# GpSimd's order around the first norm: the second value-weight load ahead of the power, two casts behind the next pair's x

## The chip, the cores and the metric

The kernel runs on one core of a Trainium2 chip. The metric is the device time of one execution in microseconds. A core has five engines with a queue of instructions each, worked off in order: TensorE (PE, with its weight loads as PEld), VectorE (DVE), ScalarE (ACT), GpSimd (POOL) and SyncE (SP). They wait for one another through semaphores. DMA transfers are issued from a queue (here SP's, ACT's or POOL's) and then run by themselves on 16 DMA engines.

## What is computed

The reference is a hashed attention and, on its output, a feed-forward layer with a root-mean-square norm ahead of it:

```
# attention: q, k, v are (4 batches, 8 heads, 768, 64), proj is (64, 6)
bucket(t) = sum_j 2**j * (t @ proj > 0)[j]              # for q and for k
scores = where(q_bucket == k_bucket, q @ k.T / 8, -1e9)
attn = softmax(scores) @ v
# feed-forward: x is (3072, 512), d_ff is 1536
xn = x / sqrt(mean(x * x) + 1e-6) * rms_g
g, val = xn @ w_gate, xn @ w_val
out = (g * sigmoid(g) * val) @ w_out
```

Input and output are float32.

## The kernel before

**Units and steps.** The work is cut into eight units u: four batches, and two halves of 384 queries each. Within a unit there are eight heads, and each head has three steps, so 24 steps (`NS`) make a unit. One list, `order`, gives the heads' order; units 0 and 1 (batch 0) start interleaved. In every step, the kernel issues the two score matmuls of the step after (`scores`, L335, s_ps), the exponential of this step on ScalarE (`probs`, L347, psb), and then whatever stands in `plan[step]`.

**The order is written out by hand.** `at(w, s, f, ...)` appends a call to `plan[24 * w + s]`; within one step calls run in the order in which `at` was called. Nothing is reordered afterwards, so this order is the order of instructions in each engine's queue. Semaphores then see to what waits for what.

**What lies in the steps.** `av` multiplies probabilities and v (L360, o_ps). After a pair of heads, `attn_out` adds a correction (DVE, L374), takes a reciprocal (DVE, L379), and on POOL makes x (L381) and its square (L387); for the last pair of unit 0 DVE does this itself (x on L381, three squares with their sums on L390). When a unit's eight heads are done, `norm_scale` adds the sums (DVE, L408, ss) and takes the power -1/2 on POOL (L412, rstd). `norm` multiplies the three thirds of x by it (L423, xn): DVE does all three in later units; in unit 0 it does two and ScalarE the last. `turn_x` turns each third on PE (L430, x_ps) and scales it into xnT (L436 on DVE, L434 on ScalarE for one third of unit 0). Then `gate` and `value` run through twelve column blocks of the weights (L447, g_ps and v_ps; L455 on ScalarE, L464 and L465 on DVE), spread over the following 24 steps, and `project` (L476, y_ps) and `store` follow one unit later. PE fills the wait for the first norm with a few matmuls of no use (`idle_bank`, L543, z_ps) in steps 34 to 36.

**The feed-forward weights** come in six loads on POOL's DMA queue (`load_w`, L548): the gate and the value weights by halves of their columns (wg and wv, 768 KB each), the output weights by halves of their rows (wo). PE reads the second halves of wg and wv from column block 6 on.

**q and k** of the first six pairs of heads are turned on PE (`turn_pe`); `cast_pool` then casts them to float16 into QK, on POOL in two instructions for each of q and k (L177, rows 0 to 63). The pair (1, 0), which is batch 1's first, has its q cast in step 38, the pair (1, 1) in step 41. The scores of batch 1 start in step 47. Later pairs are turned on DVE (L187, L194) from loads in small blocks (`load_blocks`, L119, on SP's queue) and cast by L207. `zero_rows` (L145) clears rows 64 to 127 of a QK buffer on POOL before it is used again. `v_prep` and `v_sum` (L303, L309 to L311) prepare v on POOL.

**POOL's queue around the first norm**, from the plan: the second half of wg (step 31), the power of unit 0 (step 31), the second half of wv (step 38), the two casts of q of pair (1, 0) (step 38), x and its square of the pair of heads 2 and 3 of unit 1 (step 38), the first half of wo (step 39), a `zero_rows` (step 39), the casts of q of pair (1, 1) (step 41), another `zero_rows` (step 41), the second half of wo (step 42), and `v_prep` and `v_sum` of two pairs (steps 42 and 43).

Of the kernel before, what the change touches and what calls it, by code (L numbers as in the profile page):

```python
# [33 lines left out]
def kernel(  # L34
# [526 lines left out]
    def at(w, s, f, *a):  # L561
        plan[NS * w + s].append(lambda: f(*a))
# [75 lines left out]
    at(0, 19, v_prep, 0, 3, nc.vector)  # L638
    for hp, t in enumerate((6, 16, 21, 28)):
        at(0, t, v_mean, 0, hp, 2, *([range(6)] if hp else []))  # L640
    for i, (t, t2) in enumerate(((22, 25), (31, 38))):
        cols = slice(i * DFF // 2, (i + 1) * DFF // 2)
        at(0, t, load_w, wg, moe_w_gate, 0, 4, cols)
        at(0, t2, load_w, wv, moe_w_val, 0, 4, cols)
        at(0, 39 + 3 * i, load_w, wo, moe_w_out, 6 * i, 6)


    for hp, ts in ((0, (8, 22, 23, 24, 25, 24, 38, 26, 28, 42)), (1, (20, 27, 28, 29, 30, 29, 41, 32, 33, 43))):
        tl, ts = ts[0], ts[1:]
        for w in "kq":  # L650
            at(0, tl, load_natural, nc.sync, 1, hp, w)
        at(0, tl, load_v, nc.sync, 1, hp)
        at(0, ts[0], new_pair, 1, hp)
        for t, hh, w in zip(ts[0:4], (0, 1, 0, 1), "kkqq"):
            at(0, t, turn_pe, 1, hp, hh, w)
        at(0, ts[4], cast_pool, 1, hp, "k")
        at(0, ts[5], cast_pool, 1, hp, "q")
        if hp == 0:
            at(0, ts[6], hash_pair, 1, hp)
            at(0, ts[7], send_pair, 1, hp)  # L660
        at(0, ts[8], v_prep, 1, hp)
        at(0, ts[8], v_sum, 1, hp)
# [24 lines left out]
    for n, (u, h) in enumerate(order):  # L687
        t = 3 * n + 4 - ((u, h) == (0, H - 1))
# [94 lines left out]
    def behind_norm(t):  # L783

        return t - t % NS + 7 if 1 <= t % NS < 7 else t

    for (b, hp), (load, kturns, qturns, _) in spots.items():
# [3 lines left out]
        for w, turns in (("k", kturns), ("q", qturns)):  # L791
            for i, t in enumerate(turns):
                at(0, t, turn_dve, b, hp, w, i, len(turns))
            t = turns[-1] + 1
            at(0, t if (b, hp) == (1, 2) else behind_norm(t), cast_pool, b, hp, w)
        t = 54 if (b, hp) == (1, 2) else behind_norm(qturns[-1] + 2)
# [66 lines left out]
```

## Time and profile before

| | us |
|---|---|
| runs of the kernel (three) | 333.89, 334.36, 334.40 |
| their median | 334.36 |
| the profiled execution | 334.42 |
| span of the profile (first to last instruction) | 332.6 |
| TensorE busy | 325.7 |
| VectorE busy | 239.5 |
| ScalarE busy | 227.2 |
| GpSimd busy | 163.7 |

The profile is of one execution. The span is what the instructions cover; the rest of the execution's time lies around it. Lines of a timeline give the start and the length in us, the engine, the line of the kernel, the operation, the output and inputs by name with partitions and elements, how many instructions were merged into the row, and in brackets how long the engine sat idle before it and what ended that. Spans of matmuls are modelled with their pipeline, so a following matmul can start before the one ahead of it has ended in the profile.

Of POOL's six weight loads the page gives issue and landing (size of each, median time from issue to landing):

```profile
wg<-in_moe_w_gate_dram POOLq DMA_DIRECT2D x2, 768.0 KB, 9.9
wv<-in_moe_w_val_dram POOLq DMA_DIRECT2D x2, 768.0 KB, 11.0
wo<-in_moe_w_out_dram POOLq DMA_DIRECT2D x2, 768.0 KB, 8.5
```

### The profile page before, as it was taken

To read this page: it belongs to the slowest core of one execution; us is meant where nothing else is said; L and a number is where in the kernel's file an instruction comes from. 1 tells how busy PE (TensorE), PEld (TensorE's weight loads), DVE (VectorE), ACT (ScalarE), POOL (GpSimd) and SP (SyncE) were. 2 spreads that over 40 slices of the span, in tenths; PEclk is the share of its full clock that TensorE was granted. 3 is DMA by queue.
4 is the path that set the end of the run, shared out by engine and by line. 5 is a ranking of instruction groups with operands and counts; after the bars stand their busy time and mean duration, and the time that the engine had idled before them with its cause. 6 is when DMAs were issued, how large, how long until landed. Compare 5 with 4: busy or idle time off the path is not lost.

```text
span 332.6 us, 7846 instructions
## 1 busy us (share of the span) xinstructions
PE 325.7 (98%) x2999; PEld 196.7 (59%) x2999; DVE 239.5 (72%) x496; ACT 227.2 (68%) x331; POOL 163.7 (49%) x210
## 2 busy tenths in 40 slices
PE   9999989999999999999999999999999999999995
PEld 3576656656565565655566565655656566665554
DVE  5887876869888669876888468886767356675860
ACT  6899876666677667676767667776766767744321
POOL 3999679955974743726583523556371111111000
PEclk9999999999999999999999999999999999999999
DMA  7942999996129655342807036001000010002002
GB/s 223 339 157 70 224 217 200 188 172 125 67 41 158 98 137 103 52 97 70 173 9 143 17 99 127 7 3 68 34 4 2 16 64 20 0 2 95 3 0 96
DMA packets 79613, 30.93 MB, mean 93 GB/s; under 512 B 64908, under 2 KB 76632, under 8 KB 79576
## 3 DMA queue, kind: packets, MB, share of 16 engines
q1 hardware_dynamic: 75672, 25.65, 32.7%
q0 software_dynamic: 3680, 4.72, 8.6%
q8 instruction: 23, 0.38, 0.5%
q14 instruction: 14, 0.11, 0.1%
q10 hardware_dynamic: 224, 0.07, 0.1%
HBM read 28.32 MB, written 6.29 MB: 104 GB/s over the span
## 4 chain that ended last, share of the span: by engine, by line
PE 92%; DVE 2%; issue 1%; ACT 1%; POOL 1%; DMA 1%; SPq 0%; POOLq 0%
PE v_ps L447 18%; PE s_ps L335 18%; PE g_ps L447 18%; PE y_ps L476 18%; PE o_ps L360 10%; PE d_ps L215 2%; PE t_ps L155 2%; PE d_ps L235 2%; PE x_ps L430 2%; PE z_ps L543 1%; ACT psb L347 1%; PE y_ps L495 1%; DMA qL<-in_q_dram 1%; PE m_ps L319 0%; DVE otmp L374 0%
## 5 line engine op out<-in xcount | busy, mean ns | idle before, releaser
L347 ACT ACTIVATE psb<-s_ps,ebias 128x768 f16<-128x768 f32 x192 | 167.7, 899 | 21.1 <-PE s_ps L335 20.0
L335 PE MATMUL s_ps<-QK 128*128 128x384 f16 (+1 forms) x384 | 93.6, 326 | 1.2 <-ACT psb L347 1.1
L455 ACT ACTIVATE t<-g_ps 128x384 f32<-128x384 f32 x96 | 47.1, 491 | 54.2 <-PE g_ps L447 53.4
L447 PE MATMUL g_ps<-xnT,wg 128*128 128x384 f16 x384 | 82.7, 326 | 0.0
L447 PE MATMUL v_ps<-xnT,wv 128*128 128x384 f16 x384 | 81.8, 326 | 0.4 <-DVE a L464 0.2
L464 DVE SCALAR_TENSOR_TENSOR a<-t,g_ps 128x384 f32<-128x384 f32 x96 | 52.8, 550 | 26.1 <-ACT t L455 24.6
L476 PE MATMUL y_ps<-wo,ht 128*128 128x512 f16 x276 | 68.1, 379 | 0.0
L381 POOL TENSOR_TENSOR x<-otmp,rcp 128x384 f32<-128x384 f32 x30 | 25.1, 836 | 84.6 <-DVE rcp L379 84.1
L465 DVE SCALAR_TENSOR_TENSOR ht<-a,v_ps 128x384 f16<-128x384 f32 x96 | 53.2, 554 | 11.6 <-PE v_ps L447 3.1
L360 PEld LDWEIGHTS <-psb 128*128 128x128 f16 x1152 | 52.0, 98 | 15.7 <-issue 1.2
L360 PE MATMUL o_ps<-vl,psb 128*128 128x65 f16 x1152 | 55.8, 193 | 0.0
L335 PEld LDWEIGHTS <-QK 128*128 128x128 f16 (+1 forms) x384 | 34.5, 98 | 34.4 <-issue 9.2
L447 PEld LDWEIGHTS <-wv 128*128 128x128 f16 x384 | 35.3, 97 | 22.6 <-issue 2.0
L447 PEld LDWEIGHTS <-wg 128*128 128x128 f16 x384 | 34.8, 97 | 20.7 <-DVE xnT L436 0.4
L476 PEld LDWEIGHTS <-ht 128*128 128x128 f16 x276 | 24.8, 98 | 22.4
L488 ACT COPY ysb<-y_ps 128x512 f32<-128x512 f32 x23 | 13.5, 586 | 19.7 <-PE y_ps L476 19.7
L387 POOL TENSOR_TENSOR sq<-x 128x384 f32<-128x384 f32 x30 | 24.8, 826 | 2.4
L207 POOL CAST QK<-qT 64x768 f16<-64x768 f32 x20 | 16.4, 821 | 18.1 <-DVE qT L194 17.0
L374 DVE TENSOR_TENSOR otmp<-o_ps,cvb 128x390 f32<-128x390 f32 x32 | 17.9, 558 | 10.3 <-PE o_ps L360 10.1
L423 DVE TENSOR_SCALAR xn<-x,rstd 128x512 f16<-128x512 f32 x23 | 16.9, 789 | 7.2 <-POOL rstd L412 7.2
L396 DVE TENSOR_REDUCE ssp<-sq 128x3 f32<-128x384 f32 x30 | 15.9, 528 | 7.9 <-POOL sq L387 7.8
L207 POOL CAST QK<-kT 64x768 f16<-64x768 f32 x20 | 16.4, 820 | 10.1 <-DVE kT L194 7.1
(83 smaller groups left out, 283.3 us busy)
## 6 DMA issues: line engine op xcount, KB each, us to landing
vn<-in_v_dram SPq DMA_DIRECT2D x16, 384.0 KB
out_dram<-ysb SPq DMA_DIRECT2D x23, 256.0 KB
qL<-in_q_dram SPq DMA_DIRECT2D x40, 96.0 KB
kL<-in_k_dram SPq DMA_DIRECT2D x40, 96.0 KB
kn<-in_k_dram SPq DMA_DIRECT2D x5, 384.0 KB
qn<-in_q_dram SPq DMA_DIRECT2D x5, 384.0 KB
wg<-in_moe_w_gate_dram POOLq DMA_DIRECT2D x2, 768.0 KB, 9.9
wv<-in_moe_w_val_dram POOLq DMA_DIRECT2D x2, 768.0 KB, 11.0
```

The source lines that it names most:

```text
L207: nc.gpsimd.tensor_copy(QK[b, 2 * hp + hh, "h"][0:64, o : o + S], src[64 * hh : 64 * hh + 64, :])
L335: nc.tensor.matmul(ps[:, j, 0:HALF], QK[b, h, "h"][rows, S + jt * 128 : S + (jt + 1) * 128], QK[b, h, "h"][rows, half * HALF : (half + 1) ...
L347: nc.scalar.activation(psb[u, h][:, 2 * ch : 2 * ch + 2, :], sps.pop((u, i))[:, :, 0:HALF], AF.Exp, bias=ebias, scale=ESCALE,)
L360: nc.tensor.matmul(o[:, c, hh, 0:65], psb[u, h][:, jt, c * 128 : (c + 1) * 128], vls[b % 2][:, h, 2 * (jt % 3) + jt // 3 if b in PARITY el ...
L374: nc.vector.tensor_add(tmp[:, :, :, 0:65], o[:, :, :, 0:65], cvb[b % 2][:, 2 * hp : 2 * hp + 2, 0:65].unsqueeze(1).to_broadcast([128, 3, 2 ...
L381: eng.tensor_mul(xd.rearrange("p c (h d) -> p c h d", h=2), tmp[:, :, :, 0:64], r.to_broadcast([128, 3, 2, 64]),)
L387: eng.tensor_mul(sq, xd, xd)
L447: nc.tensor.matmul(ps, w[:, kt, fs], xnT[u][:, kt, :], start=(kt == 0), stop=(kt == 3))
L455: nc.scalar.activation(t, fbank[u, ft, "g_ps"], AF.Tanh, scale=0.5)
L464: nc.vector.scalar_tensor_tensor(out=a, in0=t, scalar=1.0, in1=g, op0=ALU.add, op1=ALU.mult)
L465: nc.vector.scalar_tensor_tensor(out=ht[u][:, ft, :], in0=a, scalar=0.5, in1=vv, op0=ALU.mult, op1=ALU.mult)
L476: nc.tensor.matmul(y, ht[u][:, ft, c * 128 : (c + 1) * 128], wo[:, ft, :], start=(ft == 0), stop=(ft == NF - 1),)
```

## The change

Two numbers in the plan change. The second load of the value weights moves from step 38 to step 31: it stands right behind the second gate load and ahead of the power of unit 0 in POOL's queue. The two casts of q of pair (1, 0) move from step 38 to step 39: they stand behind x and its square of step 38 and behind the first load of the output weights, which was already in step 39, and ahead of the `zero_rows` of that step. Nothing else moves, and no instruction is added or removed.

```diff
-    for i, (t, t2) in enumerate(((22, 25), (31, 38))):
+    for i, (t, t2) in enumerate(((22, 25), (31, 31))):
         cols = slice(i * DFF // 2, (i + 1) * DFF // 2)
         at(0, t, load_w, wg, moe_w_gate, 0, 4, cols)
         at(0, t2, load_w, wv, moe_w_val, 0, 4, cols)
         at(0, 39 + 3 * i, load_w, wo, moe_w_out, 6 * i, 6)
 
 
-    for hp, ts in ((0, (8, 22, 23, 24, 25, 24, 38, 26, 28, 42)), (1, (20, 27, 28, 29, 30, 29, 41, 32, 33, 43))):
+    for hp, ts in ((0, (8, 22, 23, 24, 25, 24, 39, 26, 28, 42)), (1, (20, 27, 28, 29, 30, 29, 41, 32, 33, 43))):
```

## The prediction

> **What bounds the kernel.** I read the page first, then the chain of waits between 41 and 47 us, then the timeline of each engine there. The page (busy time by engine, then the shares of the chain that ended last) says that TensorE is the bound:
>
> ```profile
> PE 325.7 (98%) x2999; PEld 196.7 (59%) x2999; DVE 239.5 (72%) x496; ACT 227.2 (68%) x331; POOL 163.7 (49%) x210
> ...
> PE 92%; DVE 2%; issue 1%; ACT 1%; POOL 1%; DMA 1%; SPq 0%; POOLq 0%
> ```
>
> The granted clock is full in all 40 slices. Only what fills a hole in TensorE's stream, or opens one, moves the end. The span is 332.6 us and PE is idle for 6.9 us of it. The change touches POOL (GpSimd) around 40 to 52 us, so the next view is PE's timeline there (start, duration, line, tile, idle before it and its releaser):
>
> ```profile
> 43.20 0.48 PE L335 MATMUL s_ps<-QK 70*128 70x384 f16 x2
> 44.09 0.40 PE L430 MATMUL x_ps<-ident,xn 128*128 128x128 f16 x4 [0.40 <-DVE xn L423]
> 45.05 0.62 PE L430 MATMUL x_ps<-ident,xn 128*128 128x128 f16 x8 [0.56 <-DVE xn L423]
> ...
> 46.39 0.33 PE L447 MATMUL g_ps<-xnT,wg 128*128 128x384 f16 x1
> ```
>
> There is the hole: before the first feed-forward matmul PE waits twice, 0.40 + 0.56 = 0.96 us, for the two normalised thirds that VectorE makes (L423). DVE's timeline shows them, the same line in two later norms with three thirds each, and the scaling of the turned blocks:
>
> ```profile
> 42.94 2.06 DVE L423 TENSOR_SCALAR xn<-x,rstd 128x512 f16<-128x512 f32 x2 [0.38 <-POOL rstd L412]
> 44.92 1.27 DVE L436 TENSOR_TENSOR xnT<-x_ps,gcol 128x512 f16<-128x512 f16 x2
> ...
> 113.71 2.76 DVE L423 TENSOR_SCALAR xn<-x,rstd 128x512 f16<-128x512 f32 x3 [0.97 <-POOL rstd L412]
> ...
> 192.03 1.28 DVE L423 TENSOR_SCALAR xn<-x,rstd 128x512 f16<-128x512 f32 x3 [0.97 <-POOL rstd L412]
> ```
>
> The same instruction takes about 1.04 us here, about 0.95 at 113.7, and well under 0.5 at 192. The table by stage, taken over stretches that hold these instructions, says why (columns: PE, PEld, DVE, ACT and POOL busy, granted clock, DMA share, GB/s):
>
> ```profile
> 42.90:45.00 2.10, 1.19 (x9) 0.42 (x6) 2.06 (x3) 1.65 (x3) 2.04 (x4) 1.00 1.29 214
> ...
> 113.70:116.50 2.80, 2.80 (x26) 1.60 (x25) 2.79 (x4) 2.29 (x3) 2.64 (x4) 1.00 0.03 7
> ...
> 192.00:193.40 1.40, 1.40 (x11) 0.68 (x10) 1.37 (x4) 0.62 (x2) 0.00 (x0) 1.00 0.47 187
> ```
>
> Slow thirds go with a busy POOL (2.04 of 2.10 us, 2.64 of 2.80), at a DMA share of 1.29 and of 0.03 alike; the quick ones have an idle POOL, although DMA moves 187 GB/s beside them. So POOL's work, not the transfers, makes L423 slow. The shortest L423 of all is 0.477 us, so three in 1.28 start 0.40 apart. Last, POOL itself:
>
> ```profile
> 39.52 0.80 POOL L548 DMA_DIRECT2D wg<-in_moe_w_gate_dram  x1
> 42.02 0.89 POOL L412 TENSOR_TENSOR rstd<-ss,mhalf 128x3 f32<-128x3 f32 x1 [1.69 <-DVE gcol L562]
> 42.88 0.80 POOL L548 DMA_DIRECT2D wv<-in_moe_w_val_dram  x1
> 43.68 2.00 POOL L177 CAST QK<-qT 64x768 f16<-64x768 f32 x2
> 47.53 0.82 POOL L381 TENSOR_TENSOR x<-otmp,rcp 128x384 f32<-128x384 f32 x1 [1.85 <-DVE rcp L379]
> ...
> 52.82 1.68 POOL L177 CAST QK<-qT 64x768 f16<-64x768 f32 x2
> ...
> 57.16 0.82 POOL L548 DMA_DIRECT2D wo<-in_moe_w_out_dram  x1
> ...
> 65.73 1.70 POOL L207 CAST QK<-qT 64x768 f16<-64x768 f32 x2 [0.37 <-DVE qT L187]
> 69.44 1.70 POOL L207 CAST QK<-kT 64x768 f16<-64x768 f32 x2 [2.01 <-DVE kT L187]
> ```
>
> POOL idles 1.69 us before the power, then the second value-weight issue and the two casts fill exactly the stretch in which DVE makes the thirds.
>
> **Part 1, the weight issue.** It is one instruction of 0.80 us. Behind the gate-weight issue it runs from 40.32 to 41.12, inside the 1.69 us that POOL waits anyway; the sum of squares that the power needs (L408, 41.33 + 0.17) ends at 41.50. Price 0, if the issue takes 0.8 us as all six do here (0.75 to 1.01). Two unknowns. It now lies beside the three squares on DVE (L390, from 40.57, each reading x twice). Nearest row: the gate issue at 39.52 to 40.32 overlaps the DVE product x (L381, 39.98), which takes 0.56 there and 0.56 at 298.67 beside an idle POOL. I take 0; the dear end is that the squares wait from 40.57 until 41.12, a power 0.55 us later. The cheap end: this power starts 0.52 us after its sum, the one at 112.82 only 0.09 after (112.56 + 0.17). If that odd 0.43 went, x_ps would still stand behind the s_ps of 43.20, so no more than 0.1 to 0.2 us is to be had.
>
> As for the transfer, POOL's DMAs are queued behind each other: the first value load was issued at 33.98 and lands 11.2 us later, the second gate load is issued at 39.52 and lands 9.7 us later, at 49.2. An earlier issue only lengthens that queue, and SP's loads of the next pair (L119, issued 38.33 to 58.5) meet the same traffic. PE first reads the late columns at v_ps of 57.3; they land at 53.7 before, so nothing is gained there.
>
> **Part 2, the casts.** Two instructions leave 43.68 to 45.68. With part 1, POOL is then idle from the end of the power (42.91) until x is ready. So L423 starts at 42.94 as before and its two end at 42.94 + 0.40 + 0.48 = 43.82 in place of 45.00. The third xn is ScalarE's (43.03 + 0.73 = 43.76). PE: the s_ps of 43.20 streams 0.33, so the first x_ps goes at 43.53 for 0.22, the second at 43.82 + 0.05 = 43.87 in place of 45.05: 1.18 earlier. Then g_ps needs all of xnT. On DVE: the first x_ps ends at 43.53 + 0.40, then 1.27 for two, hence 45.25 instead of 46.19. On ScalarE, L434 can start when the exponential of 43.65 (0.91) is done, 44.56, in place of 45.71. g_ps at 45.30 in place of 46.39 is **1.09 us** earlier.
>
> Behind x and its square (47.53, 48.43) and the first output-weight issue (49.20), the casts cost what the same casts cost at 52.82: 1.68, with gaps 1.75. POOL has no pause from 47.53 to 65.36, so all behind them slides 1.75 us against PE until the pauses before 65.73 (0.37) and 69.44 (2.01) take it up: 2.38 > 1.75. Who waits in between: batch 1's first q is read by the 128-row s_ps of 64.38, 12 us after the casts would end. The second output-weight issue comes at 57.16 + 1.75 - 1.09 = 57.8 and lands in 7.4 to 9.5 us, by 67.3 at the latest; PE reads its first row block at 68.71 + 2 x 0.22 - 1.09 = 68.1. x of 63.63 and its square (end 65.36, then 67.1) feed the DVE sum of 69.21. All hidden; thinnest cover 0.8 us, at the weights. Each cast also stays clear of a DVE norm there.
>
> Sum: -1.09 us on the profiled execution of 334.42 us (span 332.6 and 1.8 around it) gives 333.33; the median of the runs is 334.36, 0.06 lower. I predict **333.3 us**.
>
> **Rivals.** *A power held by the squares.* The Trainium skill (SBUF — State Buffer, section Who interferes with whom) gives VectorE and GpSimd one port pair as an exclusive lock, also against DVE instructions with two SBUF inputs where GpSimd reads SBUF. Should the issue count as such, the squares wait. In rows: power 0.55 later, thirds done at 44.37, second x_ps at 44.42, gain 0.5 to 0.6, so 333.8 us. Against it stands the unhindered product at 39.98. Chance 0.12.
>
> *The gain is not kept.* PE is 1.1 us early, but a later step waits for something at a fixed time, a transfer. The view of waits lists one wait of PE for a load (vn, 0.6 us) and none of DVE; but DMA is full until 69 us, and slack that was never used isn't seen. Then 334.3 us. Chance 0.10.
>
> *Slower: no room in POOL's DMA queue.* At 40.32 the first gate load is not wholly in (31.30 + 10.1 = 41.4), and first value and second gate load are under way: the new issue is the fourth, where the trace never has more than three. If the issue must wait for the first value load (33.98 + 11.2 = 45.2), POOL stands still with the power behind it: rstd at about 45.5 to 46, 3.6 later, less the 1.1 us of quick thirds: 336.9 us. It decides from a wait that ends after 41.5 + 1.1 = 42.6 us. Against it: the third in flight took 0.80 to issue, the first 1.01; there is no growth. Chance 0.10.
>
> **How the numbers follow.** Forecast 0.68 (333.1 to 333.7), the rivals 0.12, 0.10 and 0.10. Differences under 0.2% (0.67 us) can't be told from none here. Faster: nearly all of the forecast and a third of the first rival, 0.70; slower: the queue, and a little of the kept-nothing case, 0.11; same: the rest, 0.19. The range 332.8 to 334.3 holds the forecast with 0.3 us for a prompt power and the scatter of three runs (333.89 to 334.4), the first rival, and half of the second: 0.85.
>
> **What would show it.** POOL: value issue near 40.3 with 0.8 us, power still at 42.0, then idle until x at about 46.4, casts near 49 to 51. DVE: two L423 in about 0.88 us. PE: no wait over 0.1 us before x_ps, g_ps near 45.3. Output weights landed before y_ps needs them, and no new PE wait up to 70 us. Wrong, if the issue takes over 1.3 us, if the thirds stay at 1 us beside an idle POOL, or if g_ps comes early and the end does not.

## The result, and the profile after

The changed kernel takes 333.13 us (median of 14 runs, 332.26 to 334.02) where the kernel before takes 333.93 us beside it (14 runs, 333.28 to 334.40). The ratio is 0.9976, with a 95% interval of 0.9966 to 0.9987: 0.8 us faster, with 0.43 to 1.14 us inside the interval. The profiled execution has a span of 331.8 us in place of 332.6.

TensorE is busy as long as before, in a shorter span. The first lines of the page of the changed kernel:

```profile
span 331.8 us, 7843 instructions
...
PE 325.6 (98%) x2998; PEld 196.8 (59%) x2999; DVE 238.5 (72%) x496; ACT 227.1 (68%) x331; POOL 163.4 (49%) x210
```

The timeline of TensorE in the changed kernel, around the first norm (start, length, line, operation):

```profile
43.27 0.48 PE L335 MATMUL s_ps<-QK 70*128 70x384 f16 x2
43.60 0.83 PE L430 MATMUL x_ps<-ident,xn 128*128 128x128 f16 x12
44.27 0.44 PE L360 MATMUL o_ps<-vl,psb 128*128 128x65 f16 x9
44.67 0.49 PE L335 MATMUL s_ps<-QK 70*128 70x384 f16 x2
44.99 0.44 PE L360 MATMUL o_ps<-vl,psb 128*128 128x65 f16 x9
45.46 0.81 PE L447 MATMUL g_ps<-xnT,wg 128*128 128x384 f16 x4
```

The twelve x_ps matmuls now stand in one piece right behind the s_ps; the two waits of 0.40 and 0.56 us are gone, and the first g_ps starts at 45.46 in place of 46.39. VectorE's timeline shows the two thirds in 0.88 us in place of 2.06, and then a new pause, now for TensorE:

```profile
42.65 0.88 DVE L423 TENSOR_SCALAR xn<-x,rstd 128x512 f16<-128x512 f32 x2
44.02 1.29 DVE L436 TENSOR_TENSOR xnT<-x_ps,gcol 128x512 f16<-128x512 f16 x2 [0.49 <-PE x_ps L430]
```

GpSimd's timeline:

```profile
40.39 0.75 POOL L548 DMA_DIRECT2D wv<-in_moe_w_val_dram  x1
41.72 0.89 POOL L412 TENSOR_TENSOR rstd<-ss,mhalf 128x3 f32<-128x3 f32 x1 [0.59 <-DVE gcol L562]
46.34 0.83 POOL L381 TENSOR_TENSOR x<-otmp,rcp 128x384 f32<-128x384 f32 x1 [3.73 <-DVE rcp L379]
...
48.94 1.72 POOL L177 CAST QK<-qT 64x768 f16<-64x768 f32 x2
...
57.75 0.82 POOL L548 DMA_DIRECT2D wo<-in_moe_w_out_dram  x1
...
65.91 1.70 POOL L207 CAST QK<-qT 64x768 f16<-64x768 f32 x2
68.49 1.70 POOL L207 CAST QK<-kT 64x768 f16<-64x768 f32 x2 [0.89 <-DVE kT L187]
```

It idles 3.73 us where it worked before, the casts follow at 48.94, and the delay they hand on is used up in the pauses before 65.91 and 68.49, of which 0.89 us is left.

**How stages are compared here.** The whole program starts sooner or later from one execution to the next: POOL's product x (L381) that starts at 36.20 in the profile before starts anywhere from 35.13 to 36.29 in the profiles of this study, though no instruction ahead of it in the program differs. So I take that product as a mark. D is the start of the first g_ps less the mark: 46.39 - 36.20 = 10.19 us before, 45.46 - 36.27 = 9.19 us after, 1.00 us less. The last y_ps matmul lies 292.68 us behind the mark before and 291.69 after, 0.99 less: the gain goes through to the end whole, and it lies inside the interval of the times. The span shows 0.84 because this execution's mark came 0.07 us later and 0.08 more passed behind the last matmul.

### The profile page after: what moved, and what is told of

The parts are those of the page before. It is cut to its first block, busy times and chain, and to the rows that moved or that the text cites. A ratio compares the mean times of both kernels' runs of the same rounds, so it can differ in the third digit from the quotient of the medians.

```text
span 331.8 us, 7843 instructions
## 1 busy us (share of the span) xinstructions
PE 325.6 (98%) x2998; PEld 196.8 (59%) x2999; DVE 238.5 (72%) x496; ACT 227.1 (68%) x331; POOL 163.4 (49%) x210
## 4 chain that ended last, share of the span: by engine, by line
PE 93%; DVE 2%; ACT 1%; POOL 1%; DMA 1%; issue 0%; SPq 0%; POOLq 0%
PE s_ps L335 19%; PE v_ps L447 18%; PE g_ps L447 18%; PE y_ps L476 17%; PE o_ps L360 10%; PE t_ps L155 2%; PE d_ps L215 2%; PE d_ps L235 2%; PE x_ps L430 2%; PE z_ps L543 1%; DVE xn L423 1%; ACT psb L347 1%; PE y_ps L495 1%; DMA qL<-in_q_dram 1%; PE m_ps L319 0%
## 5 line engine op out<-in xcount | busy, mean ns | idle before, releaser
L381 POOL TENSOR_TENSOR x<-otmp,rcp 128x384 f32<-128x384 f32 x30 | 25.1, 836 | 86.4 <-DVE rcp L379 86.0
L423 DVE TENSOR_SCALAR xn<-x,rstd 128x512 f16<-128x512 f32 x23 | 15.8, 739 | 6.8 <-POOL rstd L412 6.8
```

Source lines behind the costliest of these rows:

```text
L381: eng.tensor_mul(xd.rearrange("p c (h d) -> p c h d", h=2), tmp[:, :, :, 0:64], r.to_broadcast([128, 3, 2, 64]),)
L423: mul(xn[u][:, c, :], x[u][:, c, :], rstds[u][:, c : c + 1])
```

## The experiments

All in one table; times are medians, "one run" where a kernel was run once. "First" and "second" are the lengths of the two L423 on VectorE, "power" is from the end of its sum (L408) to its start. The kernel before ran again beside these kernels, with medians from 333.67 to 334.04 us; each ratio below is against the runs beside its own kernel, so two rows of the last column that differ by a few tenths say little.

| kernel | power, us | first, second, us | D, us | last y_ps behind the mark, us | time, us |
|---|---|---|---|---|---|
| before | 0.51 | 1.10, 1.04 | 10.19 | 292.68 | 333.93 |
| before, again | 0.52 | 1.10, 1.04 | 10.20 | 292.74 | 333.79, one run |
| changed | 0.15 | 0.49, 0.48 | 9.19 | 291.69 | 333.13 |
| load's issue alone moved | 0.15 | 1.04, 1.05 | 9.78 | 292.26 | 333.60 |
| casts alone moved | 0.50 | 0.49, 0.62 | 9.19 | 292.02 | 333.04 |
| changed, memset beside the thirds | 0.15 | 2.96, 0.47 | 12.07 | 295.18 | 336.36, one run |
| casts moved, small step ahead of the power | 0.15 | 0.49, 0.62 | 9.19 | 291.64 | 333.30, one run |
| changed, fewer fillers | 0.15 | 0.49, 0.48 | 9.19 | 291.67 | 332.86 |
| the same, third on VectorE | 0.15 | 0.49, 0.48 | 9.19 | 291.34 | 331.81, one run |
| the same (scalar third), first third turned earlier | 0.15 | 0.49, 0.48 | 9.00 | 292.37 | 333.02 |
| casts moved, small memset behind the issue | 0.52 | 0.49, 0.62 | 9.19 | 291.79 | 332.30, one run |
| casts moved, long memset behind the issue | 0.51 | 0.49, 0.62 | 9.19 | 291.65 | 332.51, one run |
| casts moved, small copy behind the issue | 0.52 | 0.49, 0.62 | 9.19 | 291.70 | 332.67, one run |
| casts moved, cast of v behind the issue | 0.52 | 1.10, 1.04 | 10.20 | 292.73 | 334.13, one run |

**1. Each half alone.** The first kernel moves only the load's issue, the second only the casts:

```diff
-    for i, (t, t2) in enumerate(((22, 25), (31, 38))):
+    for i, (t, t2) in enumerate(((22, 25), (31, 31))):
...
-    for hp, ts in ((0, (8, 22, 23, 24, 25, 24, 38, 26, 28, 42)), ...
+    for hp, ts in ((0, (8, 22, 23, 24, 25, 24, 39, 26, 28, 42)), ...
```

> Only the second value load moves ahead of the power; the casts stay in step 38, behind the power. D is the start of the first g_ps less the start of POOL's product x near 36.2 us: 10.19 us before (46.39 - 36.20), 9.19 with the whole change (45.46 - 36.27). Theory (any POOL instruction that runs holds VectorE's L423, a whole instruction at a time): the two casts run beside the thirds, L423 stays near 1.05 us each, two in about 2.0; only the prompt power (0.15 us behind its sum as with the whole change, 0.51 before) is left, D 9.8 to 9.9, time 0.3 us under before. Rival A (the load's issue alone slowed L423, the casts are harmless): two L423 in 0.9 us, D 9.2. Rival B (the prompt power has nothing to do with the issue ahead of it): power 0.5 us behind its sum, D 10.1 to 10.2.

> Only the casts move behind the next pair's x; the second value load stays behind the power. Theory: the first L423 is held until the issue's end (about 1.1 us), the second runs alone (0.4 later); two in about 1.5 us, in place of 2.06 and 0.88. Power 0.5 us behind its sum as before. D 9.6 to 9.7, time 0.5 us under before. Rival A (an issue of a load does not hold VectorE, only the casts do): two L423 in 0.9 us, D 9.2 to 9.5. Rival C (only the issue does): the same as the theory here, told apart by the run with the issue alone moved.

With the issue alone moved, the casts start right behind the power, and both thirds stay slow: each ends 0.28 to 0.29 us behind the end of a cast (43.00 behind 42.71, 43.97 behind 43.68). GpSimd's and VectorE's timelines of that kernel:

```profile
41.04 0.89 POOL L412 TENSOR_TENSOR rstd<-ss,mhalf 128x3 f32<-128x3 f32 x1 [0.59 <-DVE gcol L562]
41.90 1.78 POOL L177 CAST QK<-qT 64x768 f16<-64x768 f32 x2
```

```profile
41.96 2.00 DVE L423 TENSOR_SCALAR xn<-x,rstd 128x512 f16<-128x512 f32 x2
```

Only the prompt power is gained: D 9.78, ratio 0.9989 (0.9980 to 0.9999), as the theory had it. The casts alone bring all of D, 9.19, and a ratio of 0.9968 (0.9956 to 0.9980). Here the theory missed: the issue beside the thirds does not hold the first (0.49), and the second only to 0.62. The two halves do not add up: 0.41 us and 1.00 us of D make 1.00 together.

In its profiled execution this kernel lost part of that again, at a place that the prediction had not looked at. TensorE's timeline there:

```profile
45.34 0.81 PE L447 MATMUL g_ps<-xnT,wg 128*128 128x384 f16 x4
46.35 0.82 PE L447 MATMUL v_ps<-xnT,wv 128*128 128x384 f16 x4 [0.20 <-DMA wv<-in_moe_w_val_dram]
```

The first v_ps should follow 0.65 us behind g_ps, at 45.99. It waits until 46.35 for the first half of the value weights, whose last DMA engine landed at 46.31, over 2 us behind the fifteen others (all in by 44.12). In the changed kernel's profile the last landing was 44.84, with v_ps at 46.10; in the other profiles without a long hole there (the memset's is left out), it lies 0.65 to 2.7 us ahead of v_ps. So an earlier norm meets a transfer that is sometimes just in time.

**2. Does any work of GpSimd hold VectorE?** The changed kernel, with a clearing of QK rows (it only writes) put beside the thirds:

```diff
-    for i, t in ((0, 39), (1, 41), (2, 57), (3, 61)):
+    for i, t in ((0, 38), (1, 41), (2, 57), (3, 61)):
```

> The whole change, and the first of the two clearings of QK rows (L145, 2.65 us, it reads nothing) is taken from step 39 to step 38, so that it runs beside the two thirds. Theory (any POOL instruction holds them): the first L423 waits for the memset's end at about 45.3, two L423 end near 46.1 to 46.2, D 11.2 to 11.5: over 1 us worse than before. Rival (only POOL instructions that read SBUF hold L423): two in 0.9 us, D 9.2.

GpSimd's timeline, then VectorE's, then TensorE's of this kernel:

```profile
41.96 2.65 POOL L145 MEMSET QK<- 64x3072 f16 x1
```

```profile
41.94 3.35 DVE L423 TENSOR_SCALAR xn<-x,rstd 128x512 f16<-128x512 f32 x2
```

```profile
42.56 0.48 PE L335 MATMUL s_ps<-QK 70*128 70x384 f16 x2
44.95 1.24 PE L430 MATMUL x_ps<-ident,xn 128*128 128x128 f16 x12 [1.90 <-DVE xn L423]
```

The first third is shown from 41.94 and ends at 44.90, 0.29 us behind the memset's end (44.61), as the thirds beside the casts ended 0.28 to 0.29 us behind theirs. The second, with GpSimd idle, takes 0.47. So it is a hold for the length of the other's instruction, not a sharing of speed, and reading SBUF is no condition. D grew more than was expected, 12.07 for 11.2 to 11.5: the rest is in the last section.

**3. Why the power is prompt.** The casts moved, and one small instruction (`tick` is a tile of one column) ahead of the power:

```diff
         at(0, t2, load_w, wv, moe_w_val, 0, 4, cols)
+        if i:
+            at(0, 31, nc.gpsimd.memset, tick, 0.0)
```

> As the run with only the casts moved, with one POOL instruction added ahead of the power: a memset of one column behind the second gate load. It asks why the power starts 0.15 us behind its sum in the changed kernel and 0.51 before. If any instruction ahead of it in the queue (another place in the instruction stream) does that: 0.1 to 0.15, and D 0.3 us under the run with only the casts moved. If it needs the load's issue there, or a pause of POOL under 1 us: 0.5, and D as in that run.

0.15 us: the one-column memset there takes as much off the power's start as the issue did (0.36 us), so it needs no load. But D is 9.19 with the power at 0.50 and at 0.15. What is behind those 0.36 us (they are there in both profiles of the kernel before) was not found.

**4. What D is made of now.** Without the two fillers (matmuls of no use) of step 36, and then with the last third on VectorE as well:

```diff
-    for t, n in ((34, 2), (35, 1), (36, 2)):
+    for t, n in ((34, 2), (35, 1)):
```

```diff
-        for c in range(3 if u else 2):
+        for c in range(3):
...
-                at(0, TX-1, norm_third, u, 2, nc.scalar.mul)
```

> The whole change, without the two matmuls of no use in step 36 (0.44 us of TensorE ahead of the last s_ps before x_ps). In the changed kernel x_ps no longer waits for its thirds but stands behind these. Theory (D of 9.19 is a floor that TensorE's own queue and ScalarE set): x_ps goes 0.4 us earlier, the first scaling on VectorE too, and then g_ps stands behind the s_ps that waits for ScalarE's exponential (it would stay near 9 us after the mark); D about 9.0, a gain of 0.15 to 0.2 us, too small for the time to show beside the changed kernel. Rival (the thirds or the weights still bound it): D stays 9.19.

> As the run without the two fillers, with the last third also made by VectorE in place of ScalarE. VectorE then makes three thirds in 1.28 us, so its scaling of xnT starts 0.4 us later than in that run, while ScalarE's exponential comes 0.6 us earlier. Theory (with the fillers gone VectorE's chain binds): D 9.05 to 9.1, no better than without the fillers alone. Rival (ScalarE binds): D 8.8 to 8.9.

The theory of both expectations fell: D stays at 9.19. The time without the fillers (332.86; 0.9968 of before, 0.9956 to 0.9980) cannot be told from the changed kernel's. The last y_ps comes 0.33 us sooner with the third on VectorE as well (291.34 for 291.67), but most of this was gained at 208 us, far from the edit, in one execution. TensorE's timeline without the fillers says why:

```profile
42.63 0.48 PE L335 MATMUL s_ps<-QK 70*128 70x384 f16 x2 [0.28 <-ACT psb L347]
42.95 0.83 PE L430 MATMUL x_ps<-ident,xn 128*128 128x128 f16 x12
```

The s_ps ahead of x_ps waits for ScalarE to free its buffer, so the fillers had only filled a wait. Its place is 42.63 - 35.63 = 7.00 us behind the mark, the same as in the changed kernel (43.27 - 36.27). From there 0.33 to x_ps, 0.42 to VectorE's first scaling (43.38), 1.29 for two, and 0.14 to g_ps at 44.81 make 9.19. To test this, the first third was turned ahead of that s_ps:

```diff
-                    at(0, TX, turn_x, u, c, c == 2)
+                    at(0, TX - (c == 0), turn_x, u, c, c == 2)
```

> The whole change without the two fillers of step 36, and the turning of the first third (four of the twelve x_ps matmuls) goes from step 37 to step 36, ahead of the s_ps that ScalarE's exponential paces. D was 9.19 in the changed kernel, without the fillers, and with a third moved to VectorE alike. Theory (D is that s_ps, 7.00 us behind the mark, 0.33 of it, 0.4 for the first x_ps, 1.29 for VectorE's two scalings and 0.15 to g_ps): the first scaling starts 0.4 us earlier and D falls to 9.0, where the next s_ps and o_ps ahead of g_ps hold it; time as with the changed kernel within what a run can tell (0.2 us of 333). Rival (something else fixes g_ps, such as the weights): D 9.19 again.

D is 9.00, as the theory said, the only one here under 9.19. Its time (333.02; 0.9969 of before, 0.9955 to 0.9983) cannot be told from the changed kernel's (0.9976). In its profiled execution the 0.19 us held until 82 us and were then lost, with 0.7 us more, around a hole of TensorE, 0.76 us long before the s_ps of 83.70, that no other profile has. The profile puts it down to ScalarE's exponential for the matmul and to the queue itself ("issue") for the weights. What it was stays open.

**5. Why the first third was slow behind the issue.** With the casts behind it, the issue of a load goes with a first L423 of 1.10 us; with nothing behind it, 0.49. The kernel before was profiled again, and three other things were put behind the issue: a memset of one column, the long memset, a copy of one column; and last the cast of v (L303), moved from step 42:

```diff
-        at(0, ts[8], v_prep, 1, hp)
+        at(0, ts[8] if hp else 38, v_prep, 1, hp)
```

> The kernel before, once more with a profile. If the first L423 beside the issue and the queued casts is slow by the order of instructions: 1.0 to 1.1 us again, two in 2.0 to 2.1, the power 0.5 us behind its sum, D 10.1 to 10.2. If it was chance: a first of 0.49 us, D 9.6 to 9.8. The last landing of the first value load (45.21 us there, 46.31 in the run with only the casts moved) should vary by a microsecond between executions.

> As the run with only the casts moved (first L423 0.49, second 0.62 us beside the issue of a load), with a memset of one column (0.12 us) queued right behind that issue. It asks why the first L423 took 1.10 us in the kernel before, although the casts are shown to start after it should have ended. Theory (an instruction queued behind the issue already holds VectorE back): first L423 1.0 to 1.1 us, two in 1.4 to 1.5. Rival (only a cast does, or the profile's start of the cast is late): first 0.49, second 0.6 to 0.75.

> As the run with only the casts moved, with the clearing of QK rows (L145, 2.65 us) behind the issue of the second value load, where the casts stood in the kernel before. Theory (POOL's next long instruction already holds VectorE while the issue is shown): the first L423 takes over 2.5 us, D above 11.5. Rival (an instruction holds from where the profile shows its start, here about 43.7; the casts before did something of their own): first L423 0.49 us, the second waits for the memset's end, about 46.3; D about 12.

> As the run with the small memset behind the issue, with a copy of one column (it reads SBUF) in its place. The first L423 was 1.10 us with casts queued behind the issue, and 0.49 with nothing, with a small memset and with a long one there. Theory (a POOL instruction that reads SBUF takes hold while the issue ahead of it is still shown): first L423 0.8 to 1.1 us, the issue under 0.8. Rival (length matters, or the cast's own form): first 0.49, second 0.62, issue 0.86.

> As the run with only the casts moved, with the cast of batch 1's first v (L303, 128 by 768, alone 0.82 us) taken from step 42 to behind the issue. Theory (a long POOL instruction that reads SBUF takes hold while the issue is still shown): first L423 1.0 to 1.1 us, the second waits for the cast and ends near 45, D 10.1 to 10.2, as before. Rival (only the casts of q did): first 0.49, second 0.62, D 9.2.

The kernel before repeats its thirds and D to 0.01 us, so it was no chance (the first value load landed 1.4 us earlier against the program's start, at 43.80 in place of 45.21). Both memsets and the small copy leave 0.49 and 0.62. With the long memset neither side of the expectation held whole: the second third did not wait for it. The cast of v brings back 1.10, 1.04 and D 10.20. GpSimd's and then VectorE's timeline with the long memset behind the issue:

```profile
42.02 0.86 POOL L548 DMA_DIRECT2D wv<-in_moe_w_val_dram  x1
42.92 2.77 POOL L145 MEMSET QK<- 64x3072 f16 x1
```

```profile
42.08 1.02 DVE L423 TENSOR_SCALAR xn<-x,rstd 128x512 f16<-128x512 f32 x2 [0.38 <-POOL rstd L412]
```

and the same two with the cast of v there, the first third alone and then both:

```profile
42.53 0.80 POOL L548 DMA_DIRECT2D wv<-in_moe_w_val_dram  x1
43.33 1.03 POOL L303 CAST vl<-vn 128x768 f16<-128x768 f32 x1
```

```profile
42.59 1.10 DVE L423 TENSOR_SCALAR xn<-x,rstd 128x512 f16<-128x512 f32 x1 [0.39 <-POOL rstd L412]
...
42.59 2.06 DVE L423 TENSOR_SCALAR xn<-x,rstd 128x512 f16<-128x512 f32 x2 [0.39 <-POOL rstd L412]
```

With the memset, the issue is the one that stretches (0.86 us) and VectorE goes through; the memset itself then takes 2.77 where it takes 2.65 elsewhere. With the cast, the issue keeps its 0.80 and VectorE's first third waits. But it does not wait for the cast: it ends at 43.69, 0.36 us behind the issue's end (43.33) and 0.68 ahead of the cast's (44.37), and the cast takes 1.03 where it takes 0.82 alone. The kernel before shows the same: its first third ends at 44.04, 0.36 behind the issue's end (43.67), and the first of its casts takes 1.03. The second third ends 0.29 us behind that cast in both.

So with a long cast queued behind it, the issue of a load goes with a first third that lasts until just past the issue's end; with a memset, a short copy or nothing behind it, it does not. That the cast already takes hold while the issue is still shown would be one reading, but its own 1.03 us and its late end speak against it. What the cast changes in the issue, these runs cannot show. One cast is enough; the kernel before had two.

## Why the prediction was right

**Direction, place and size** held: 333.13 us against 333.3, and 1.00 us at the first g_ps against the forecast 1.09. That the times lie only 0.17 us apart is in part luck: the forecast took 1.06 us off a median of three runs, 334.36, and the runs show 0.80 us off a median of 333.93.

**What bounds it, and the cause.** TensorE's hole before the norm, filled by quick thirds: two L423 in 0.88 us as forecast, beside an idle GpSimd. That GpSimd's work and not the transfers slows L423 was read from rows at other norms, and the moved memset showed it: the third grew from 0.49 to 2.96 us beside it.

**Where the 0.09 us went.** The mis-sized term is the last step, from VectorE's second scaling to g_ps. I had put 0.05 us, although the rows before have 46.39 - 46.19 = 0.20 there; it is 45.46 - 45.31 = 0.15. My terms ahead of it also do not add up as written: 43.53 + 0.40 + 1.27 is 45.20, not 45.25. The slip made up for two terms that were a little short: the first scaling starts 0.42 us behind x_ps, and the two take 1.29.

**Part 1** was priced at nothing, and nothing is what it is worth once the casts are moved: D is 9.19 with and without it, and the times cannot be told apart. (With the casts left in place it gave 0.41 us of D.) I had noted the odd 0.43 us of the power and that the s_ps ahead of x_ps would swallow it. It did go (0.36), and it was swallowed. But my sentence that the issue and the casts together fill the stretch made the issue share the blame. Without casts behind it, it has little: it costs 0.14 us on the second third, which ends nowhere near the path. With them, the first third did last until just past its end, so for that third the rows before cannot part the two; moving the casts freed both thirds.

**Part 2** carries the whole gain. Its price behind x was sized right: the second output-weight issue at 57.75 (forecast 57.8), and the slide gone by the cast of 68.49. The output weights landed at 66.92, and TensorE read the row block in question at 68.01: 1.1 us of cover, where I had 0.8.

**What was overlooked:** the thinnest cover was not there but at the first half of the value weights, read by the first v_ps. I checked only its second half. In one profile of a kernel with the casts moved, this cost 0.36 us of the gain.

**The rivals.** *Power held by the squares*: the three L390 lie beside the issue in the changed kernel and take 0.29 us as before, with the power earlier, not later. *No room in the DMA queue*: the fourth load in flight was issued in 0.75 us, though the first gate load landed 0.35 us after that issue began; with the third on VectorE as well it landed 1.28 us after, and the issue took 0.75 us too. *Gain not kept*: 0.99 of 1.00 us arrive at the last y_ps in the changed kernel; as a risk it was real, by way of the late landing above.

## What to carry to other kernels

Ahead of a wait on the critical engine, look at what a neighbour that is off the path runs beside the instruction that ends the wait; the same line at another place, with that neighbour idle, gives its price without a run. When two edits at one place each shorten another input of a join, try each alone: only the last input counts, and here one edit was worth everything and the other nothing on top of it. And compare short stages from a mark inside the program, since starts varied by 1.2 us where the change is worth 0.8.

## What was not expected of the hardware

**A hole of about 2 us, and then half the clock on TensorE.** In the one execution of the kernel with the memset beside the thirds, TensorE had 0.10 us of work in 43 to 45 us. The table by stage (PE, PEld, DVE, ACT and POOL busy, then the granted clock, DMA share, GB/s):

```profile
43.00:45.00 2.00, 0.10 (x2) 0.05 (x2) 2.00 (x2) 0.92 (x2) 1.61 (x1) 1.00 1.33 221
45.00:46.00 1.00, 1.00 (x13) 0.84 (x14) 0.90 (x3) 0.00 (x0) 0.00 (x0) 0.79 1.34 222
46.00:47.00 1.00, 1.00 (x13) 0.78 (x12) 0.68 (x2) 0.77 (x4) 0.00 (x0) 0.50 1.26 210
47.00:48.00 1.00, 1.00 (x13) 0.71 (x11) 0.14 (x1) 1.00 (x3) 0.00 (x0) 0.50 1.30 214
48.00:49.00 1.00, 1.00 (x5) 0.49 (x4) 0.61 (x2) 0.16 (x1) 0.21 (x1) 0.50 1.30 216
49.00:50.00 1.00, 1.00 (x8) 0.61 (x7) 0.34 (x1) 0.86 (x2) 0.92 (x2) 1.00 1.30 216
```

The clock, 0.79 on average from 45 to 46 us, fell to half some 0.6 us after the hole had ended, and stayed there until 49. The matmuls bear it out: the first four of g_ps take 1.47 us there and 0.81 in the changed kernel. The wait of about 2 us became a loss of 2.88 us at g_ps and 3.49 at the last y_ps, against the changed kernel. The Trainium skill (TensorE: Matmul & The Clock Gate, Part 1) gives an idle window of about 3.4 us for this; here the clock fell behind a hole of 1.90 us without a matmul, and the measurement stands. The kernel before, with holes of 0.40 and 0.56 us, kept its full clock. That the hole caused the fall is read from their order in one execution.

**The hold goes by whole instructions.** The Trainium skill (SBUF — State Buffer, section Who interferes with whom) says of GpSimd and a VectorE instruction in a two-port mode that the second to issue blocks until the first is done. The memset of 2.65 us and the third that ended 0.29 us behind it agree. Both are shown to start within 0.03 us of each other (41.94 and 41.96), so the trace does not tell which issued first. That L423 is in such a mode no run here shows.

GpSimd waits in its turn: behind the issue and a third that was not held, the one-column memset takes 0.26 us where it takes 0.12 ahead of the power, and ends 0.03 us behind the second third.
